# Zero fills of two stages issued in pairs, 2 MB to one transfer, in a DMA-bound decode kernel

## The chip, the cores and the metric

The kernel runs on one core of one Trainium2 chip. Times are device microseconds (us) of that core, the median of several executions; profiles are of one execution each. Every run reported here was classed as undisturbed ("fast"), so like is compared with like. The profile's column PEclk is the share of its full clock that TensorE was granted: 1.00 in most of the stages discussed here, 0.50 in the lines from 330 us on. A transfer's landing time is the time from its issue to its arrival. The backlog is what has been issued and has not landed yet.

## The reference, cut to what matters

One token goes through a conditioned transformer block, and the kernel returns the block's output and the gradients of all ten differentiated inputs. Two of these are large: the gradients of the two key and value caches, of 4 heads x 65,536 rows x 128 each.

```python
def _A_ref(x, k_cache, v_cache, wq, wo):          # Hkv, Sk, Dh = 4, 65536, 128
    W = min(4096, max(256, Sk // 4))              # 4096: only the last 4096 rows are read
    ...
    k = jnp.repeat(k_cache[:, :, Sk - W:, :], rep, axis=1)
    v = jnp.repeat(v_cache[:, :, Sk - W:, :], rep, axis=1)
    ...
def reference(...):
    _out, _vjp = jax.vjp(_f, A_x, A_k_cache, A_v_cache, A_wq, A_wo, B_w_gate, B_w_up, B_w_down, c, w_mod)
    return (_out0, *[jnp.asarray(_g) for _g in _vjp(grad_out)])
```

The first 61,440 rows of each head of both cache gradients are zeros: some 126 MB of the 186 MB that the kernel writes. Those writes are the zero fills.

## The kernel before

The fills are cut into 120 regions of about 1 MB. Eight of them are "narrow", in a shape that leaves out eight rows; the others are plain. The function `zero(n, after)` issues the next n of them on GpSimd's DMA queue, each after some matmul, so that TensorE's progress paces them. Lists say how many are issued at each step of each stage. N and B are the code's names for two stages of large matmuls (tiles n_ps and b_ps below). In B the same queue also carries 1 MB loads of the weight w_mod, and a short step, called ga, makes 64 small matmuls with a part of it.

```python
Z_N = spread(29, 128)                       # N stage: 29 fills over 128 steps
Z_B = spread(29, 43) + [1, 1, 1, 1, 0]      # B stage: 33 fills over 48 chunks
...
    ZW = 4096
    zeros = vt([P, ZW // 2], "zeros", FP8)  # 128 rows x 2 KB of zeros
...
    def zero(n, after=None):
        for _ in range(n):
            ...
            region, narrow_ = zleft.pop(0)
            ...
            else:
                ins = nc.gpsimd.dma_start(out=region.bitcast(FP32), in_=zeros[:, :])
            if after is not None:
                dep(first or ins, after)
...
            for k in range(2):              # N stage, step s of 128
                mm = nc.tensor.matmul(nbank[k][:, :], ...)
            zero(Z_N[s], recent(mm, 6))
...
            for a in range(4):              # B stage, one chunk of 48: 8 matmuls
                for k in range(2):
                    mm = nc.tensor.matmul(bbank[p][k][:, :], ...)
            zero(Z_B[nbq - 1 - len(bq)], recent(mm, 3))
...
    keep[0] = 0
    zero(len(zleft))                        # what is left, at the very end
```

After B comes the FFN loop: seven turns that load weights, form gradients in place, store them, and issue four or more fills each.

## Time and profile before

| | kernel before |
|---|---|
| time, median (lowest to highest) | 607.25 us (607.07 to 607.41), 3 runs |
| span of the profiled run | 605.6 us |
| bytes moved | 248.19 MB, mean 410 GB/s |
| TensorE busy | 388.1 us (64%) |
| N stage, B stage, FFN loop from | 75, 157 and about 293 us |

How to read it: a row such as GB/s of the page cuts the span into 40 slices of 15.1 us. In a kernel that is bound by transfers every slice should be near the best one; a lower slice is time lost, unless its transfers are of a slower kind. The view of stretches gives the same for any cut. The prediction shows these lines for the kernel before, with the waits and the order of GpSimd's instructions.

### The profile page before, as it was taken

To read this page: it belongs to the slowest core of one execution; us is meant where nothing else is said; L and a number is where in the kernel's file an instruction comes from. 1 tells how busy PE (TensorE), PEld (TensorE's weight loads), DVE (VectorE), ACT (ScalarE), POOL (GpSimd) and SP (SyncE) were. 2 spreads that over 40 slices of the span, in tenths; PEclk is the share of its full clock that TensorE was granted. 3 is DMA by queue.
4 is the path that set the end of the run, shared out by engine and by line. 5 is a ranking of instruction groups with operands and counts; after the bars stand their busy time and mean duration, and the time that the engine had idled before them with its cause. 6 is when DMAs were issued, how large, how long until landed. Compare 5 with 4: busy or idle time off the path is not lost.

```text
span 605.6 us, 10906 instructions
## 1 busy us (share of the span) xinstructions
PE 388.1 (64%) x4496; PEld 265.6 (44%) x4516; DVE 325.1 (54%) x616; ACT 282.4 (47%) x426; POOL 177.8 (29%) x281
## 2 busy tenths in 40 slices
PE   3997788999899989989450454344343277757200
PEld 3995434334344446648340353333333256656200
DVE  3754498999511010060462866756667288778420
ACT  3489514557211014228181768558385833764100
POOL 0002121221322212313342464364542523132230
PEclk9999699999999989989755555555555585755555
DMA  8999999999999999999999999999999999999997
GB/s 353 419 417 421 409 426 413 413 419 420 420 425 426 424 426 419 402 425 411 403 412 391 374 396 409 407 416 404 409 414 420 420 423 411 421 424 425 426 416 282
DMA packets 49522, 248.19 MB, mean 410 GB/s; under 512 B 5629, under 2 KB 5629, under 8 KB 29056
## 3 DMA queue, kind: packets, MB, share of 16 engines
q0 software_dynamic: 37792, 210.78, 90.4%
q1 hardware_dynamic: 11632, 36.71, 17.6%
q8 instruction: 35, 0.57, 0.4%
q14 instruction: 15, 0.12, 0.1%
q10 hardware_dynamic: 48, 0.01, 0.0%
HBM read 61.87 MB, written 185.60 MB: 409 GB/s over the span
## 4 chain that ended last, share of the span: by engine, by line
PE 35%; DMA 29%; DVE 17%; ACT 8%; issue 7%; POOL 1%; ACTq 0%; POOLq 0%; another core or an unknown queue 0%; DVEq 0%; SPq 0%
DMA out_dram<-arena 15%; PE b_ps L687 14%; DMA arena<-in_B_w_down_dram 9%; PE n_ps L635 6%; DVE arena L206 4%; DVE arena L193 4%; DMA arena<-in_B_w_gate_dram 3%; DVE arena L210 3%; DVE junk L210 3%; ACT arena L241 2%; PE t_ps L597 2%; DMA arena<-in_B_w_up_dram 2%; PE tp_wq L453 2%; PE w_ps L394 2%; PE tp_k L434 1%
## 5 line engine op out<-in xcount | busy, mean ns | idle before, releaser
L169 POOL DMA_DIRECT2D out_dram<-zeros x112 | 61.6, 550 | 203.8 <-PE q_ps L471 50.4
L687 PE MATMUL b_ps<-arena 128*128 128x512 bf16 x372 | 88.2, 389 | 0.6
L836 PE MATMUL tp_side<-ident_bf,arena 128*128 128x128 bf16 x416 | 50.1, 297 | 50.9 <-ACT arena L837 41.9
L837 ACT COPY arena<-tp_side 128x1024 bf16<-128x1024 bf16 x52 | 52.1, 1010 | 56.6 <-PE tp_side L836 56.4
L193 DVE TENSOR_TENSOR arena<-arena 128x2048 bf16<-128x2048 bf16 x64 | 76.5, 1224 | 2.3 <-PE n_ps L635 0.3
L210 DVE CUSTOM_DVE_ANT_0 arena<-arena,scr 128x1024 bf16<-128x1024 bf16 x56 | 65.2, 1222 | 9.4 <-ACT scr L969 9.4
L635 PE MATMUL n_ps<-arena 128*128 128x512 bf16 x248 | 65.0, 378 | 7.0 <-DVE arena L193 5.1
L836 PEld LDWEIGHTS <-arena 128*128 128x128 bf16 x416 | 41.1, 137 | 56.2 <-issue 56.1
L241 ACT ACTIVATE arena<-scr,h 128x1024 bf16<-128x1024 bf16 x56 | 61.0, 1145 | 0.0
L687 PEld LDWEIGHTS <-arena 128*128 128x128 bf16 x384 | 37.7, 100 | 46.5 <-issue 7.1
L210 DVE CUSTOM_DVE_ANT_0 junk<-arena,b1k 128x1024 bf16<-128x1024 bf16 x28 | 34.3, 1224 | 26.9 <-DMA arena<-in_B_w_down_dram 26.4
L873 POOL DMA_DIRECT2D out_dram<-arena x42 | 30.7, 734 | 45.8 <-ACT arena L241 38.1
L635 PEld LDWEIGHTS <-arena 128*128 128x128 bf16 x256 | 24.6, 97 | 41.8 <-issue 16.4
L1134 ACT ACTIVATE arena<-ps_kv 128x512 bf16<-128x512 f32 x48 | 26.2, 687 | 28.4 <-PE ps_kv L1130 28.2
L599 ACT CAST arena<-t_ps 128x512 bf16<-128x512 f32 x56 | 30.1, 589 | 12.1 <-PE t_ps L597 12.1
L1130 PE MATMUL ps_kv<-junk,arena 8*128 8x128 bf16 x256 | 26.9, 303 | 11.6 <-DVE arena L206 10.3
L949 PE MATMUL fg<-hh_bf,arena 128*128 128x1 bf16 x224 | 8.1, 166 | 40.5 <-DMA arena<-in_B_w_down_dram 38.8
L1130 PEld LDWEIGHTS <-arena 8*128 8x128 bf16 x256 | 25.0, 140 | 13.3 <-issue 13.3
L202 DVE CAST arena<-b_ps 128x512 bf16<-128x512 f32 x5 | 3.5, 692 | 47.1 <-PE b_ps L687 47.1
L949 PEld LDWEIGHTS <-arena 128*128 128x128 bf16 x224 | 7.1, 105 | 43.5 <-DMA arena<-in_B_w_down_dram 41.4
L455 ACT COPY arena<-tp_wq 128x1024 bf16<-128x1024 bf16 x23 | 21.8, 1032 | 8.1 <-PE tp_wq L453 8.1
L206 DVE TENSOR_SCALAR arena<-arena,cs_col 128x4096 bf16<-128x4096 bf16 (+1 forms) x16 | 16.0, 1017 | 8.2 <-DMA out_dram<-arena 8.0
(297 smaller groups left out, 650.7 us busy)
## 6 DMA issues: line engine op xcount, KB each, us to landing
out_dram<-zeros POOLq DMA_DIRECT2D x112, 1024.0 KB, 13.8
out_dram<-arena POOLq DMA_DIRECT2D x32, 1024.0 KB, 18.9
out_dram<-arena POOLq DMA_DIRECT2D x36, 512.0 KB, 9.3
arena<-in_A_wq_dram SPq DMA_DIRECT2D x8, 1024.0 KB, 19.9
out_dram<-zeros POOLq DMA_DIRECT2D x8, 960.0 KB, 12.7
arena<-in_B_w_down_dram SPq DMA_DIRECT2D x14, 512.0 KB, 10.6
out_dram<-arena POOLq DMA_DIRECT2D x28, 256.0 KB, 10.3
arena<-in_A_wo_dram SPq DMA_DIRECT2D x6, 1024.0 KB, 25.0
```

The costliest lines, as they stand in the source:

```text
L169: ins = nc.gpsimd.dma_start(out=region.bitcast(FP32), in_=zeros[:, :])
L193: return nc.vector.tensor_tensor(out=out, in0=a, in1=b, op=op)
L206: return nc.vector.tensor_scalar(out=out, in0=a, scalar1=s1, scalar2=None, op0=op0)
L210: return nc.vector.tensor_tensor_reduce(out=out, in0=w, in1=b, scale=1.0, scalar=0.0, op0=ALU.mult, op1=ALU.add, accum_out=acc)
L241: return nc.scalar.activation(out=out, in_=b, func=ACT.Copy, scale=col)
L599: nc.scalar.copy(out=o, in_=ps)
L635: mm = nc.tensor.matmul(nbank[k][:, :], lhsT=k_nat[:, g, t_ * DH:(t_ + 1) * DH], rhs=vp[:, t_ % 2, 4 * k:4 * k + 4, :].rearrange("p h d -> ...
L687: mm = nc.tensor.matmul(bbank[p][k][:, :], lhsT=a4[:, p, h, :], rhs=wo_t[u][:, a, k * 512:(k + 1) * 512], start=(i == 0 and a == 0), stop= ...
L836: nc.tensor.transpose(tp[:, i * P:(i + 1) * P], blk[:, i * P:(i + 1) * P], ident_bf[:, :])
L837: nc.scalar.copy(out=blk, in_=tp[:, :])
L873: nc.gpsimd.dma_start(out=ug_part(view, q, j0, n), in_=ug_tile(q, k, j0, n))
L1130: nc.tensor.matmul(ps[:, t4 * DH:(t4 + 1) * DH], lhsT=rows[32 * g:32 * g + HG, t_ * P:(t_ + 1) * P], rhs=hd[32 * g:32 * g + HG, :], start= ...
```

## The change

The intent is fewer and larger transfers in the N and B stages. A fill there takes two neighbouring regions when it can, and the lists are cut to 17 and 18 calls.

```diff
-Z_N = spread(29, 128)
-Z_B = spread(29, 43) + [1, 1, 1, 1, 0]
+Z_N = spread(17, 128)
+Z_B = spread(16, 43) + [1, 0, 1, 0, 0]
...
+    def wide_fill(region, i, n):
+        return nc.gpsimd.dma_start(
+            out=region[:, i * ZW:(i + n) * ZW].bitcast(FP32).rearrange("p (t x) -> p t x", t=n),
+            in_=zeros[:, :].rearrange("p (t x) -> p t x", t=1).broadcast_to([P, n, ZW // 2]))
...
-    def zero(n, after=None):
+    def zero(n, after=None, most=1):
...
             else:
-                ins = nc.gpsimd.dma_start(out=region.bitcast(FP32), in_=zeros[:, :])
+                m = 1
+                while m < most and zleft and not zleft[0][1] and zleft[0][0][0] is region and zleft[0][0][1] == i + m:
+                    zleft.pop(0)
+                    m += 1
+                ins = wide_fill(region, i, m)
...
-            zero(Z_N[s], recent(mm, 6))
+            zero(Z_N[s], recent(mm, 6), 2)
...
-            zero(Z_B[nbq - 1 - len(bq)], recent(mm, 3))
+            zero(Z_B[nbq - 1 - len(bq)], recent(mm, 3), 2)
...
-    zero(len(zleft))
+    zero(len(zleft), None, 2)
```

More of the change, by code (lines that the diff above doesn't have):

```diff
@@ L127 @@
             for i in range(region.shape[1] // ZW):
-                zregions.append(region[:, i * ZW:(i + 1) * ZW])
+                zregions.append((region, i))
     narrow = zregions[0:len(NARROW)]
@@ L156, in zero @@
                 return
-            region, narrow_ = zleft.pop(0)
+            (region, i), narrow_ = zleft.pop(0)
             first = None
@@ L165, in zero @@
                 ins = nc.gpsimd.dma_start(
-                    out=region[8:P, :].bitcast(FP32).rearrange("(t p) x -> p t x", t=2),
+                    out=region[8:P, i * ZW:(i + 1) * ZW].bitcast(FP32).rearrange("(t p) x -> p t x", t=2),
                     in_=zeros[0:60, :].rearrange("p (t x) -> p t x", t=1).broadcast_to([60, 2, ZW // 2]))
             else:
-                ins = nc.gpsimd.dma_start(out=region.bitcast(FP32), in_=zeros[:, :])
+                m = 1
[3 more added lines that the diff above has]
+                ins = wide_fill(region, i, m)
             if after is not None:
```

## The prediction

> **What bounds the kernel now.** I read the page's slices first, then the DMA table, the waits, the stretches (busy time and DMA rate by window), the landing times of the fills, and the order in time of GpSimd's instructions. The page:
>
> ```profile
> GB/s 353 419 417 421 409 426 413 413 419 420 420 425 426 424 426 419 402 425 411 403 412 391 374 396 409 407 416 404 409 414 420 420 423 411 421 424 425 426 416 282
> HBM read 61.87 MB, written 185.60 MB: 409 GB/s over the span
> out_dram<-zeros POOLq DMA_DIRECT2D x112, 1024.0 KB, 13.8
> ```
>
> Between start and drain no slice falls below 374 GB/s and the best reach 426, so the transfers bound the whole kernel: 248.19 MB at 426 GB/s would be 583 us of the 605.6 us span. The other 23 us are the start, the drain at the end, one dip, and stages whose mix of transfers runs at about 408. The zero fills are nearly half of the bytes. They depend on no result, so they are the ballast that keeps the queue full while compute has nothing to store. The stretches show where the rate is lost (columns: stretch, length, busy time and count of PE, PE loads, DVE, ACT, POOL, granted clock, DMA share, GB/s):
>
> ```profile
> 170.00:180.00 10.00, 9.95 (x47) 4.54 (x47) 0.08 (x2) 0.00 (x0) 2.65 (x5) 1.00 1.13 427
> 250.00:260.00 10.00, 8.42 (x110) 5.26 (x109) 0.85 (x6) 0.76 (x2) 3.00 (x6) 0.99 1.10 397
> 330.00:340.00 10.00, 4.84 (x64) 3.98 (x63) 8.04 (x18) 3.41 (x4) 5.22 (x8) 0.50 0.87 324
> 340.00:350.00 10.00, 4.33 (x79) 4.00 (x79) 7.88 (x14) 9.95 (x11) 3.27 (x6) 0.50 1.07 394
> ```
>
> The N stage (75 to 157 us) and the B stage (157 to 270 us) are PE-bound and DMA-full at once: 9.95 of 10 us of PE beside 427 GB/s. The dip of 330 to 350 us costs, against 420, 10 x (1 - 324/420) + 10 x (1 - 394/420) = 2.9 us. It lies at the first turn of the FFN loop. The waits of GpSimd, then its order in time at the stage border and at the dip:
>
> ```profile
> POOL out_dram L169 <- PE n_ps L635: 44.5, 20, 3.9
> POOL out_dram L169 <- PE b_ps L687: 36.6, 13, 7.5
> POOL out_dram L169 <- DMA out_dram<-zeros: 29.0, 17, 2.1
> ```
>
> ```profile
> 81.58 0.56 POOL L169 DMA_DIRECT2D out_dram<-zeros  x1 [3.87 <-PE n_ps L635]
> ...
> 187.90 0.53 POOL L169 DMA_DIRECT2D out_dram<-zeros  x1 [2.15 <-DMA out_dram<-zeros]
> ...
> 280.26 0.77 POOL L869 DMA_DIRECT2D arena<-in_B_w_up_dram  x1 [5.88 <-PE fold_ps L882]
> ...
> 306.13 0.72 POOL L859 DMA_DIRECT2D out_dram<-arena  x1 [1.15 <-DMA arena<-in_B_w_gate_dram]
> ...
> 333.43 0.71 POOL L859 DMA_DIRECT2D out_dram<-arena  x1 [9.04 <-DVE arena L206]
> ```
>
> Fills are released by the PE's pace in N and in most of B. The 29.0 us are another wait: in the built program GpSimd's transfers take eight completion semaphores in turn, so a transfer waits until the eighth before it has landed ("slots" below). From 180 to 213 us and from 285 to 306 us that limit holds. A fill issued in N, B or the FFN's start lands 9 to 19 us later; so the queue holds 5 to 8 MB.
>
> **What the Trainium skill says.** "DMA: Bandwidth & Descriptors", section "Anatomy of one DMA — SWDGE (gpsimd) path", fits one transfer as about 2.0 us fixed plus bytes over 436 GB/s, and says that the fixed part is mostly the wait for the write receipt. The trace agrees that it is hidden: fills of 1 MB follow each other every 2.5 us from 185 to 210 us (1.05 MB / 426 GB/s = 2.46 us). So pairing cannot save 2 us per transfer. The same page, "Issuing engines are not separate DMA queues", says that transfers of all engines share the same 16 DMA engines; the trace agrees, as SyncE's 1 MB loads of wo take 25 and 31 us beside the fills in the N stage. Its section "Bandwidth" advises batches of at least 1 MiB; both versions keep to that, so it promises little here.
>
> **The change part by part.**
>
> Removed: I replayed the lists of fills. Before, N calls 29 fills and B 33, plus the unchanged 3 of the ga step: 29 and 36 MB. After, N makes 17 calls (11 pairs, 3 singles, 3 of the narrow kind) = 28 MB, and B makes 18 (13 pairs, 3 singles, 2 narrow) = 31 MB, plus 3. With 2 pairs at the very end this makes 26 pairs, and 86 wide transfers in place of 112. At 0.534 us each that is up to 26 x 0.534 = 14 us less issue time, but GpSimd is busy 29% and off the path: worth 0. Cost inside the DMA engines: I estimate an upper bound from the gap between the page's fabric ceiling of 435 GB/s and the 427 seen with 1 MB fills; if all of that were per transfer, it would be 2% of 2.46 us = 0.05 us, and 26 x 0.05 = 1.3 us gained. I take half, **-0.6 us**.
>
> Unchanged: bytes. Each pair still writes 8 KB pieces from a 2 KB source row; the total of 120 regions stays.
>
> Moved: N and B issue 62 - 59 = 3 MB less, which go to the end (1 MB left over before, 4 MB after). 3 x 1.05 MB / 0.426 = 7.4 us of queue. By itself this is zero: what the queue does not carry at 270 us it carries at 590 us, if it runs dry in neither case. So the sum is made of dry moments:
>
> (a) N start. Before, fills come after steps 4, 8, 13, 17 of the stage; after, at 7, 15, 22. At 82.75 us (step 15) only one fill has been added where two were. The fill at 81.58 us landed 9.1 us later: less 2.0 us fixed and 2.5 us for itself, 4.6 us of queue stood ahead. Without the fill at 77.13 us, and 1.2 us later, that is 4.6 - 2.5 - 1.2 = about 0.9 us when the 2 MB are issued, and they need about a microsecond to begin. A dry moment of 0 to 1 us: **+0.4 us**.
>
> (b) B's end. The fill at 265.23 us landed after 13.5 us, so 9 us of queue stood ahead. After, the backlog is 3 MB = 7.4 us shorter from there: when the loads of gate and up are issued at 280.26 us (landing 11.1 us for 0.5 MB, so about 7.8 us ahead) some 0.4 us are left, and around 270 us it can touch zero. **+0.7 us**.
>
> (c) FFN start. Those loads land about 7 us sooner, but the first matmul that needs them started at 292.85 us, after folds that end at 291.6, so this gains only 1.5 us of compute. More comes from the slots: the first store of w_down's gradient was computed at 300.2 us and issued at 306.13, because eight transfers were outstanding. With a shorter queue it goes at about 299 and lands at about 311 in place of 319; the next w_down load follows it and lands near 321 in place of 329.84. The 10.90 us that VectorE waits there shrink to about 3, as its gates are ready at 318.5. The store that ends the dip goes near 324 in place of 333.4: 9 us sooner, for a queue 7.4 us shorter. Of the dip's 2.9 us I expect 2 back: **-2.0 us**.
>
> (d) FFN and end. Turns of the loop stay DMA-bound (about 25.5 us for 10.5 MB), earlier by 7 to 9 us. The last pairs run as the final drain, so the 3 MB come back there, +7.4 us, which cancels the shorter queue.
>
> Sum: -0.6 + 0.4 + 0.7 - 2.0 = -1.5 us, so 607.25 becomes about **605.7 us**.
>
> **The rivals.** First, the queue runs dry in B or N: lumps of 2 MB, then gaps of up to 8 us (GpSimd waited 7.5 us for the PE around 220 us) on a queue 2 to 7 us shorter. For it: step (b) leaves almost nothing at 270 us, and a dry microsecond is never earned back in a kernel bound by transfers. Against it: the backlog was 12.5 us of landing time even at its lowest in mid B. It would make 608 to 611 us. Second, fewer slots taken: with up to 16 MB instead of 8 MB outstanding, GpSimd never stalls on slots, loads go out on time, and slices of 402 to 411 GB/s in B's end and the FFN start rise to 420. For it: 17 such waits. Against it: while it waits on a slot the queue is full by definition, so nothing is lost there directly. With the whole dip and these slices recovered, 601 to 603 us. Third, pure ballast: all is hidden and the total of bytes decides, 607 us. Fourth, a deeper SWDGE queue starves the loads: in B's middle the same bytes stand ahead of the w_mod loads as before (13 MB by the second of them in both versions, N's 1 MB aside), so I give this little weight.
>
> **Range and chances.** The DMA total fixes the time within about 1%: all losses that I can name in the stages concerned are 3.4 us (dip 2.9, 250 to 260 us 0.5), and the possible new dry moments are of the same size. 8 in 10: 602.3 to 608.9. Faster by over 2% needs 595 us, more than all these losses; slower by over 2% needs 12 us of new dryness. Chances: 0.02, 0.97, 0.01.
>
> **What the profile after would show.** Bytes equal at 248.2 MB. Slots: GpSimd's 29.0 us of waits on earlier fills down to below 12. Step (b): landing times near 265 us of about 7 to 9 us, and gate and up loads at 280 us landing in 4 to 6 us. Step (c): the stretch 320 to 345 us without a 10 us piece below 360 GB/s, and the store of 306.13 us near 299. Step (d): the last fills issued near 585 us with the queue still full, and a drain like today's. Step (a) is wrong if 80 to 90 us stays at 425 GB/s. The sum is wrong if B's end shows a piece below 350 GB/s (first rival), or if the FFN turns take less than 25 us, which would mean that they were bound by waits and not by bytes.

## The result

| | before | changed |
|---|---|---|
| median of 6 runs each | 607.29 us | 612.58 us |
| lowest to highest | 606.51 to 607.41 | 610.16 to 614.35 |
| ratio, 95% interval | | 1.0087, 1.0058 to 1.0115 |
| profiled run: time, span | 607.40, 605.6 us | 610.53, 608.8 us |

The ratio is the mean time of one kernel's fast runs over that of the other's of the same rounds, so it isn't quite the ratio of the medians. The changed kernel is slower by 0.9%, outside the predicted range (602.3 to 608.9). Its runs also scatter over 4.2 us, where those of before lie within 0.9 us. The profile is of one of the quicker runs of the changed kernel, so it shows 3.1 us of the median's 5.3.

The page of the changed kernel, the lines that answer to those of before:

```profile
GB/s 354 419 416 421 405 426 411 412 421 420 421 428 426 423 410 386 404 360 395 395 418 406 385 404 413 406 412 411 410 415 420 424 416 415 424 423 426 420 415 291
HBM read 61.87 MB, written 185.60 MB: 407 GB/s over the span
out_dram<-zeros POOLq DMA_DIRECT2D x60, 1024.0 KB, 11.2
out_dram<-zeros POOLq DMA_DIRECT2D x26, 2048.0 KB, 15.6
```

The bytes are the same. Slices 16 to 20 (228 to 304 us) hold new losses: 386, 404, 360, 395, 395 where before had 419, 402, 425, 411, 403. The stretches of the changed kernel, with the columns of the same view in the prediction:

```profile
220.00:230.00 10.00, 9.56 (x61) 5.32 (x62) 1.73 (x5) 4.45 (x7) 2.24 (x3) 0.83 1.06 387
230.00:240.00 10.00, 10.00 (x100) 5.97 (x99) 0.00 (x0) 4.34 (x5) 1.45 (x2) 1.00 1.06 374
270.00:280.00 10.00, 9.08 (x164) 8.23 (x162) 0.00 (x0) 8.45 (x12) 1.93 (x4) 1.00 1.03 343
330.00:340.00 10.00, 4.50 (x40) 3.75 (x38) 8.57 (x18) 6.60 (x7) 3.70 (x6) 0.50 1.03 381
...
268.00:270.00 2.00, 1.05 (x13) 0.65 (x12) 0.59 (x1) 1.07 (x2) 1.20 (x2) 1.00 0.83 303
270.00:272.00 2.00, 1.55 (x25) 1.31 (x23) 0.00 (x0) 1.91 (x3) 1.17 (x3) 1.00 0.75 147
272.00:274.00 2.00, 1.54 (x22) 1.29 (x22) 0.00 (x0) 2.00 (x4) 0.00 (x0) 1.00 1.06 340
```

From 268 to 274 us the queue ran dry and filled again: (303 + 147 + 340) x 2 us is 1.58 MB where 425 GB/s would have moved 2.55, a loss of 2.3 us. The loss of 220 to 240 us is of another kind: the DMA share stays at 1.06. In pieces of 1 us from 227 to 235 us it is 0.83 to 1.16, at only 254 to 406 GB/s. So the queue was thin there and never quite empty; group 3 comes back to this. The dip of the FFN's first turn is smaller than before (381 for 324), as predicted. GpSimd in order of time, before the two holes and at the FFN's start:

```profile
216.75 0.70 POOL L154 DMA_DIRECT2D out_dram<-zeros  x1 [6.35 <-PE b_ps L696]
226.48 0.78 POOL L347 DMA_DIRECT2D arena<-in_w_mod_dram  x1 [9.03 <-PE b_ps L696]
...
261.90 0.72 POOL L154 DMA_DIRECT2D out_dram<-zeros  x1 [8.31 <-PE b_ps L696]
268.80 0.77 POOL L347 DMA_DIRECT2D arena<-in_w_mod_dram  x1 [6.18 <-PE b_ps L696]
...
300.67 0.72 POOL L868 DMA_DIRECT2D out_dram<-arena  x1 [1.64 <-DVE arena L215]
...
328.24 0.71 POOL L868 DMA_DIRECT2D out_dram<-arena  x1 [6.82 <-DVE arena L215]
```

For 6 to 9 us GpSimd has nothing to issue, as it waits for TensorE's next chunks. The same gaps are there in the kernel before (7.5 us ahead of its fill at 226.37 us), but with more queue behind them. The fill at 261.90 us landed after 10.1 us, at 272.0; nothing went in behind it until 268.80.

The accounts agree. From 220 to 300 us the eight 10 us stretches of before add up to 3312 GB/s and those of the changed kernel to 3108: 204 x 10 us = 2.04 MB, at 420 GB/s 4.9 us lost. From 300 to 350 us the changed kernel moves 60 x 10 us = 0.6 MB more, 1.4 us won back. The difference of 3.4 us is close to the 3.1 us by which the profiled runs differ. Why other runs lose some 2 to 4 us more, this profile doesn't show.

### The profile page after: what moved, and what is told of

Its sections match the earlier page's. It is cut to its first block, busy times and chain, and to the rows that moved or that the text cites.

```text
span 608.8 us, 10875 instructions
## 1 busy us (share of the span) xinstructions
PE 386.7 (64%) x4516; PEld 265.0 (44%) x4516; DVE 325.8 (54%) x616; ACT 282.5 (46%) x426; POOL 169.4 (28%) x255
## 4 chain that ended last, share of the span: by engine, by line
PE 35%; DMA 30%; DVE 17%; ACT 7%; issue 6%; POOL 1%; ACTq 0%; POOLq 0%; DVEq 0%; SPq 0%
DMA out_dram<-arena 15%; PE b_ps L696 14%; DMA arena<-in_B_w_down_dram 9%; PE n_ps L644 6%; DVE arena L215 4%; DVE arena L202 4%; DVE arena L219 3%; DVE junk L219 3%; DMA out_dram<-zeros 2%; PE t_ps L606 2%; ACT arena L250 2%; DMA arena<-in_B_w_gate_dram 2%; PE w_ps L403 2%; PE tp_wq L462 2%; PE tp_k L443 1%
## 5 line engine op out<-in xcount | busy, mean ns | idle before, releaser
L154 POOL DMA_DIRECT2D out_dram<-zeros x86 | 52.0, 606 | 191.3 <-PE q_ps L480 50.9
L662 ACT ACTIVATE arena<-n_ps 128x512 bf16<-128x512 f32 x8 | 4.3, 594 | 34.5 <-PE n_ps L659 34.5
```

The source lines that it names most:

```text
L154: return nc.gpsimd.dma_start(out=region[:, i * ZW:(i + n) * ZW].bitcast(FP32).rearrange("p (t x) -> p t x", t=n), in_=zeros[:, :].rearrang ...
```

## The experiments

Theory: what costs time is the amount. By B's end 3 MB less have been issued, so the queue has no backlog when GpSimd has nothing to issue. Rivals: the 2 MB transfers themselves; their lumpy placing; the queue at the FFN's start and not inside B; TensorE as the bound in B. All results below were correct against the reference. "This" and "before" ran on the same chip within one group.

### Group 1: pairs, lumps or amount

**Every pair split.** The changed kernel, but two transfers of 1 MB at the place of each pair.

```diff
-                ins = wide_fill(region, i, m)
+                ins = wide_fill(region, i, 1)
+                for x in range(1, m):
+                    wide_fill(region, i + x, 1)
```

> The changed kernel, with every pair issued as two 1 MB transfers back to back at the same place: same amounts by stage, same lumps, no 2 MB transfers. Theory (the queue runs dry in B because less is issued, in lumps): it stays slow, 609.5 to 613 us, with dry pieces near 232 us and 271 us. Rival (a 2 MB transfer itself is slower or disturbs the loads): back to 606.5 to 608 us.

Measured: 612.13 us, before 607.2, ratio 1.0084 (1.0061 to 1.0107). The loss stays without any 2 MB transfer in it, with a hole of 308 GB/s from 270 to 280 us. The size of the transfer isn't the cause.

**Fewer single fills.** The kernel before, with the changed kernel's amounts.

```diff
-Z_N = spread(29, 128)
-Z_B = spread(29, 43) + [1, 1, 1, 1, 0]
+Z_N = spread(28, 128)
+Z_B = spread(28, 43) + [1, 0, 1, 1, 0]
```

> The kernel before, with single fills, but 28 in N and 31 in B in place of 29 and 33, as the changed kernel has it; 4 single fills are left for the end. Theory in the form 'the amount does it': 609 to 612 us, a dry piece below 350 GB/s near 270 us. In the form 'the lumps do it': 606.5 to 608.5 us.

Measured: 612.3 us, ratio 1.0084 (1.0062 to 1.0105), scatter 3 us. Without pairs and without lumps, taking 1 MB from N and 2 MB from B costs what the whole change costs. The stretches of this run:

```profile
220.00:230.00 10.00, 8.82 (x57) 4.95 (x58) 2.40 (x10) 3.73 (x6) 1.84 (x3) 0.83 1.11 412
260.00:270.00 10.00, 9.21 (x38) 3.89 (x37) 9.32 (x16) 0.96 (x2) 1.55 (x3) 0.89 0.99 358
270.00:280.00 10.00, 8.92 (x145) 8.07 (x145) 0.00 (x0) 7.97 (x13) 1.85 (x4) 1.00 0.95 311
```

The hole at B's end is there and deeper; the one at 220 to 240 us is almost gone (412, and 414 in the next stretch). So the lumps move some of the loss to the middle of B, but the total is set by the amount.

**Pairs with the amount put back.** 30 MB in N and 33 in B.

```diff
-Z_N = spread(17, 128)
-Z_B = spread(16, 43) + [1, 0, 1, 0, 0]
+Z_N = spread(18, 128)
+Z_B = spread(17, 43) + [1, 0, 1, 0, 0]
```

> The changed kernel with 18 calls in N and 19 in B: 30 and 33 MB in pairs, so 1 MB more by the end of B than before the change, nothing left for the end. If the amount does it: 605 to 608 us and no piece below 390 GB/s near 270 us. If lumps or pairs do it: 609 to 613 us still.

Measured: 607.08 us, ratio 0.9996 (0.9981 to 1.0011). The loss is gone and the pairs are still there; from 270 to 280 us it moves 421 GB/s. One piece, 250 to 260 us, is at 361; it doesn't show in the time.

**The changed kernel again**, unedited, as the anchor.

> The changed kernel again on this chip, as the anchor, and to see whether its spread (610 to 614 us over six runs, against 606.5 to 607.4 before) comes again. Theory: 610 to 614 us, spread over 2 us; a profile taken in a slower run shows longer dry pieces in B than the first profile (2.3 us near 271 us).

Measured: 611.1 us (610.3 to 614.8), ratio 1.0084 (1.0051 to 1.0117). The size of the loss and the scatter repeat. The profile fell on the quickest run again, so the slow runs remain unseen.

### Group 2: how much, and where

**One MB less.** Pairs, 28 MB in N and 33 in B: the changed kernel with one more call in B, `Z_B = spread(17, 43) + [1, 0, 1, 0, 0]`.

> Pairs, 28 MB in N and 33 in B: 1 MB less than before the change by B's end. Theory (only the amount counts, and the kernel before had about 1 MB to spare: 3 MB = 7.4 us of queue cost 5.1 us in the run with fewer single fills): 607 to 608.5 us. Rival (each missing MB costs its 2.46 us, nothing was to spare): 609 to 610 us. Rival (pairs cost something of their own): also above 609 us.

Measured: 607.26 us, ratio 0.9998 (0.9983 to 1.0013). It differs from the changed kernel by one call, so 2 MB, in B alone (the other calls of B move by a step or so), and the whole loss is gone. N's missing megabyte is harmless with B's amount in place.

**Six MB less.** Single fills, 28 in N and 28 in B (`Z_B = spread(25, 43) + [1, 0, 1, 1, 0]` in the kernel before).

> Single fills, 28 MB in N and 28 in B: 6 MB less than before. Theory: 6 x 2.46 = 14.8 us of queue less the 2.3 us to spare, so about 619.5 us (617 to 621), with dry pieces in B far longer. Rival (the FFN's start takes in the gap by starting sooner, so the loss saturates): 611 to 615 us.

Measured: 620.2 us, ratio 1.0213 (1.0186 to 1.0241). The stretches:

```profile
220.00:230.00 10.00, 8.05 (x46) 4.07 (x47) 2.67 (x13) 3.93 (x7) 1.56 (x3) 0.83 0.75 262
270.00:280.00 10.00, 8.14 (x127) 7.26 (x126) 0.08 (x1) 8.22 (x13) 2.37 (x4) 1.00 0.84 280
```

From 3 MB less (612.3) to 6 MB less (620.2) the loss grows by 7.9 us, 2.6 us for each megabyte, about its full price of 2.46 us at 426 GB/s. The loss doesn't saturate.

**Three MB more.** Pairs, 32 MB in N and 33 in B (`Z_N = spread(19, 128)` in the changed kernel), taken from the end.

> Pairs, 32 MB in N and 33 in B: 3 MB more than before by B's end, taken from the end. Theory (a full queue can't gain): 606 to 607.5 us, as the run with 30 and 33 MB. If a thicker cushion also takes away the losses left in 250 to 260 us and 330 to 350 us: 604 to 605.5 us. If loads behind a deeper queue start late: 608 to 611 us.

Measured: 607.31 us, ratio 1.0007 (0.999 to 1.0024). Nothing is gained above the amount of before. This run shows best that TensorE isn't the bound in B. The first matmuls of the FFN loop in order of time, first of the changed kernel, then of this one:

```profile
291.87 1.74 PE L941 MATMUL fg<-h_bf,arena 128*128 128x1 bf16 x64
```

```profile
300.02 0.29 PE L941 MATMUL fg<-h_bf,arena 128*128 128x1 bf16 x4
```

TensorE reaches the FFN 8 us later than in the changed kernel (it also waits 5.0 us for a weight load behind the deeper queue), and the kernel ends 5 us sooner.

**Late.** The changed kernel with the missing 3 MB issued at B's end: `Z_CB = 6` in place of 3.

> The changed kernel with the 3 missing MB issued at the end of B (6 single fills in place of 3 after the last w_mod load), so that the FFN starts behind the same amount as before. If what counts is the queue at the FFN's start: 606.5 to 608 us. If what counts is the dry pieces inside B (near 232 us and 271 us, some 3.4 us in the first profile of the changed kernel), which this can't fill: 609.5 to 612 us.

Measured: 612.58 us, ratio 1.0092 (1.0071 to 1.0113). Adding the bytes behind the holes doesn't help: all six fills go out from 270.13 us, and the hole is there already.

```profile
268.00:270.00 2.00, 1.08 (x5) 0.39 (x4) 1.14 (x2) 1.07 (x2) 0.62 (x1) 1.00 0.94 348
270.00:272.00 2.00, 1.77 (x29) 1.65 (x29) 0.00 (x0) 1.33 (x2) 2.00 (x5) 1.00 0.54 74
272.00:274.00 2.00, 1.38 (x23) 1.14 (x20) 0.00 (x0) 2.00 (x3) 1.32 (x3) 1.00 0.95 334
```

The time is lost inside B, before 274 us. What goes first after the gap is the w_mod load of 269.38 us. In pieces of 1 us the rate from 271 to 275 us is 111, 319, 348 and 283 GB/s, and then 467 as the fills follow.

Together, by the amount issued up to B's end, against the kernel before:

| MB | kernel | median us |
|---|---|---|
| +3 | pairs, 32 and 33 | 607.31 |
| +1 | pairs, 30 and 33 | 607.08 |
| 0 | before, single | 607.2 |
| -1 | pairs, 28 and 33 | 607.26 |
| -3 | pairs (the change), pairs split, single | 611.1 to 612.6, 612.13, 612.3 |
| -6 | single, 28 and 28 | 620.2 |

### Group 3: TensorE's time in B, and the dip of the FFN's first turn

**Tripled small matmuls**, in the kernel before and in the changed one. They write the same result again.

```diff
     mod_tiles(ga_ps, ga_t, range(KD), True)
+    mod_tiles(ga_ps, ga_t, range(KD), True)
+    mod_tiles(ga_ps, ga_t, range(KD), True)
```

> The kernel before, with the 64 small matmuls of the ga step done three times over (same result), so that TensorE takes 3.5 us longer in the middle of B (1.74 us each in the trace). Theory: the queue's cushion at 265 us (about 9 us) hides it: 606.8 to 608.5 us. Rival (TensorE's own time is the bound in B, the transfers follow it): about 610.7 us.

> The changed kernel with the same 3.5 us more of TensorE in B. Theory: with the queue dry, each microsecond of TensorE in B is a microsecond more of the whole, 614.5 to 617 us (3 to 4 us above the changed kernel's 611 to 612.6). Rival (the loss is in the transfers alone): 611 to 613 us.

Measured: 619.18 us (ratio 1.0211, 1.0181 to 1.0242) and 624.49 us (1.0291, 1.0275 to 1.0306). Both went up by about 12 us, so both theories missed: the experiment did something else than planned. TensorE in order of time, the kernel before with the tripled matmuls:

```profile
214.85 2.18 PE L344 MATMUL ga_ps<-cs_bf,arena 128*128 128x1 bf16 x79
227.21 1.10 PE L344 MATMUL ga_ps<-cs_bf,arena 128*128 128x1 bf16 x36 [10.17 <-issue]
```

TensorE stood still for 10.17 us in the midst of the added matmuls, for nothing that the view of waits shows ("issue"). Its next step came at 231.5 us where it was at 216.0: 15.5 us of delay, not 3.5. That is more than either backlog could hide, so the pair tells nothing of the cushion. I did it again in group 4 with wide matmuls. The view of transfers by window has a lead on the stop: in both traces one packet of 16 KB of the queue that the profile calls "instruction" falls into it, at 224.7 us here and at 222.8 us in the changed kernel, each time 2.5 us before TensorE goes on (227.21 and 225.34 us). That fits instructions that came late; it was not tested.

The stop also shows how a queue empties and fills again. GpSimd had nothing to issue for 18.76 us:

```profile
232.04 0.53 POOL L169 DMA_DIRECT2D out_dram<-zeros  x1 [18.76 <-PE tot_ln_mean L255]
```

```profile
226.00:227.00 1.00, 0.00 (x0) 0.00 (x0) 0.00 (x0) 0.00 (x0) 0.00 (x0) 0.50 1.07 401
229.00:230.00 1.00, 1.00 (x4) 0.43 (x3) 0.11 (x1) 0.00 (x0) 0.00 (x0) 0.50 0.50 188
231.00:232.00 1.00, 1.00 (x5) 0.73 (x4) 0.00 (x0) 0.00 (x0) 0.00 (x0) 0.50 0.00 0
232.00:233.00 1.00, 1.00 (x4) 0.32 (x3) 0.57 (x4) 0.00 (x0) 0.53 (x1) 0.55 0.00 0
233.00:234.00 1.00, 1.00 (x6) 0.48 (x5) 0.00 (x0) 0.00 (x0) 0.00 (x0) 1.00 1.02 393
234.00:235.00 1.00, 1.00 (x7) 0.46 (x5) 0.00 (x0) 0.00 (x0) 0.47 (x1) 1.00 1.22 459
...
245.00:246.00 1.00, 1.00 (x11) 0.58 (x9) 0.00 (x0) 0.61 (x1) 0.64 (x2) 1.00 1.03 348
248.00:249.00 1.00, 1.00 (x6) 0.49 (x5) 0.00 (x0) 0.83 (x1) 0.00 (x0) 1.00 0.88 233
```

The rate falls over some five microseconds, and the DMA share with it: I read this as the 16 engines running out one after another. So a backlog loses time before it is empty. The way back is short when a fill goes first: issued at 232.04 us, it moves at 393 GB/s from 233 us and at 459 from 234. It is slow for the two w_mod loads that follow a second gap. From 245 to 251 us they move at 213 to 393 GB/s while the engines count as busy (0.87 to 1.03). The same two loads, behind a full queue in the kernel before, move at 393 to 434 GB/s (234 to 242 us). The slow stretches of the changed kernel and of the late run are such loads too: of the packets, 221 of 222 (231 to 234 us) and 189 of 190 (271 to 274 us) are under 8 KB, the size of the fills' pieces. Why a load is slow there is not shown.

**Fills ahead of the blocked store.** In the FFN's first turn GpSimd waits for VectorE with a store, and the fill behind that store waits too. Here fills go first; with pairs (on the kernel with 28 and 33 MB) and with single fills (on the kernel before: `zero(2)` for the line shown).

```diff
             if q + 2 < NB:
                 load_ug(q + 2, 0, 4)
+            if q == 0:
+                zero(1, None, 2)
             wd_outer(q + 1, 0)
-            zero(z[2])
+            if q > 0:
+                zero(z[2])
```

> Pairs with 28 and 33 MB (607.26 us), and in the first turn of the FFN loop one pair of fills issued ahead of the store that GpSimd waits for (the dip of 330 to 350 us) in place of one single fill behind it. If the dip's 2.9 us are a loss of the whole kernel: 604.5 to 606 us and no piece below 390 GB/s there. If the loop takes them back anyway: 607 to 608 us.

> The kernel before with the same step: in the first turn of the FFN loop two single fills ahead of the store that GpSimd waits for. As the run with pairs: 604.5 to 606 us if the dip is a loss of the whole, 607 to 608 us if not. If slots matter there, it gains less than the run with pairs, as its two fills wait for slots.

Measured over five rounds: 606.52 us (ratio 0.9989, 0.9976 to 1.0001) and 605.91 us (0.9981, 0.9968 to 0.9993), before 606.96. The stretches of the run with single fills:

```profile
330.00:340.00 10.00, 3.76 (x43) 2.92 (x41) 6.85 (x16) 3.30 (x4) 4.55 (x7) 0.50 1.11 414
340.00:350.00 10.00, 4.21 (x75) 3.88 (x75) 8.00 (x14) 9.95 (x11) 3.23 (x6) 0.50 1.07 412
```

The dip of 324 and 394 GB/s is filled. Of its 2.9 us only about 1 shows in the time; in this profile the piece from 250 to 260 us is lower than before (348 GB/s for 397), which would account for 1.2 us of the rest. The single fills are the one version here that is faster than both kernels clear of noise, by 0.2%; the pairs' gain isn't clear of noise.

### Group 4: TensorE's time in B again

Sixteen wide matmuls into an unused tile after the ga step, on the kernel before, on the changed one, and on the one with 3 MB more. The failed step of the prediction is about just this.

```diff
     cp(ga, ga_ps[:, 0:KD])
+    idle = psum.tile([P, 512], FP32, name="idle", tag="mm")
+    for _ in range(16):
+        nc.tensor.matmul(idle[:, :], lhsT=ident_bf[:, :], rhs=wo_t[0][:, 0, 0:512], start=True, stop=True)
```

> The run with tripled small matmuls stalled TensorE for a further 10 us in a way that the profile does not explain (some 15.4 us of delay, not 3.5), so it is done again with 16 wide matmuls into an unused tile after the ga step: 16 x 0.216 us = 3.5 us more of TensorE in B, on the kernel before. Theory: the cushion hides it, 606.8 to 608.5 us. Rival (TensorE's time in B is the bound): 610 to 611 us.

> The changed kernel with the same 3.5 us of wide matmuls. Theory: nothing hides them, 614 to 617 us. Rival: 611 to 613 us.

> Pairs with 32 and 33 MB (607.31 us) with the same 3.5 us of wide matmuls. Theory: hidden behind a thicker cushion, 606.8 to 608 us. If the place of the fills matters and not the cushion: as the kernel before with wide matmuls, or worse.

(The delay of the tripled run was 15.5 us, not the 15.4 of the first of these texts.) This time the delay is as planned: the step after it came at 219.7 us in place of 216.1 on the kernel before, and at 218.2 in place of 214.5 on the changed one.

| on | ratio to before, without | with 3.6 us more of TensorE | difference |
|---|---|---|---|
| before | 1 | 1.0027 (1.0006 to 1.0049), 609.02 us | 1.6 us |
| changed | 1.0084 to 1.0087 | 1.0126 (1.0111 to 1.0141), 614.88 us | 2.5 us |
| 3 MB more | 1.0007 | 1.0023 (1.0009 to 1.0038), 608.59 us | 1.0 us |

The order is the theory's: the thinner the queue, the more of TensorE's delay comes through. But the theory had expected the two with a full queue to hide it all, and they don't (609.02 against 606.8 to 608.5; 608.59 against 606.8 to 608). The kernel before shows a new hole at 250 to 260 us, 324 GB/s where it had 397. So its backlog isn't 9 us thick everywhere: the gap of 5.86 us ahead of the w_mod load (at 249.5 us, here at 253.1) uses it up. The kernel with 3 MB more has such a hole too: 366 and 338 GB/s from 250 to 270 us, where it had 393 and 415 without the delay. The intervals of the three differences, 1.3 to 1.8 us each way, overlap; the grading is likely, not proven.

## Why the prediction was wrong, point by point

**What bounds the kernel** was right: transfers, with equal bytes. In the profiled pair the stretches with a lower rate account for the loss (3.4 us for 3.1).

**The step that failed is (b), B's end, "a backlog 3 MB shorter can touch zero: +0.7 us".** In the profiled run, 260 to 300 us lost 3.0 us (127 x 10 us = 1.27 MB at 420 GB/s). Another 1.9 us went from 220 to 240 us, for which the sum had no term; together they are the 4.9 us above, and the median has 2 us more. Three things were wrong. First, it compared the backlog at two moments, 265 and 280 us, where a fill or load is issued. The queue runs out between issues, in the gaps of 6 to 9 us in which GpSimd waits for TensorE. At the moment of issue nothing is seen of it: the gate and up loads issued from 280.96 us landed after 6.9 to 8.2 us, later than the 4 to 6 foreseen, so the queue stood fuller than predicted, 7 us after the hole. Second, "touching zero" was priced at next to nothing. The late run moved 348, 74 and 334 GB/s in three pieces of 2 us: the queue runs out gradually, and the load that goes first is slow. Third, the same question was asked of the middle of B only in a rival. That rival named the very gap (7.5 us near 220 us), but the prediction set it aside, as 12.5 us of landing time seemed enough; less the 2 us fixed and the fill's own 2.5 us that it counts elsewhere, and 4.9 us for the 2 MB missing by then, 3.1 us were left for a gap of 9 us, and 220 to 240 us fell to 387 and 374 GB/s. The size of the queue was read too large in the same way: landing times of 9 to 19 us, less the 2 us fixed, are 3 to 7 MB at 426 GB/s and not 5 to 8.

**Step (d), that the 3 MB cost nothing as the FFN would run 7 to 9 us sooner**, failed with it. In the last turn of the loop, the last matmul that writes fg from h_bf began at 444.7 us in place of 448.8: 4.1 us sooner. The 7.4 us of fills at the end came in full; 7.4 - 4.1 = 3.3 us is the profiled loss. The single fills with 3 MB less show the same without pairs (445.5 us there, so 7.4 - 3.3 = 4.1 us, and its profiled run lost 4.3).

**Step (a)** was wrong by its own test, without harm: 76 to 88 us stays at 425 GB/s, so the dry microsecond at N's start didn't come. That a transfer needs about a microsecond to begin is borne out by the tripled run (issued at 232.04 us, nothing moved before 233).

**Step (c)** was right in kind and near in size. The first store went at 300.67 us (299 predicted, 306.13 before), the one that ends the dip at 328.24 (324 predicted, 333.43 before), and 1.4 us came back of the 2.0 expected. That the dip's time is worth less to the whole than its size was not foreseen: filled entirely, its 2.9 us gave about 1 us in the run with single fills.

**The saving per transfer** (-0.6 us) can't be seen: three kernels with pairs at 28 to 32 MB in N and 33 in B lie at ratios of 0.9996, 0.9998 and 1.0007, intervals of 0.15 to 0.17% each way, so 1 us. It is neither shown nor refuted.

**The slots** fell as predicted (GpSimd's waits of fills on earlier fills: 29.0 us before, 8.0 after) and gave nothing, as the second rival's counter-argument said. The first rival came true, with its sign of a piece below 350 GB/s at B's end (343 from 270 to 280 us); its size, 608 to 611 us, was also short.

**Open**: the scatter of 4 us. The kernels with 3 or 6 MB less scatter by 3 to 4.5 us, those with 1 MB less or with more by 1.5 us at most (1.9 to 2.6 us when TensorE is delayed in group 4). The clocks give a lead. Take each run's time and mean granted clock against the mean of its own batch. Over the 26 runs of kernels with 3 or 6 MB less the two go together (correlation -0.80, some 2.9 us more for each 0.01 of clock less); over the 30 runs of the kernel before in the four groups they don't (-0.04). That fits TensorE losing some time to the throttle, which a backlog hides. It is a correlation and not an experiment: no profile fell on one of the slowest runs, and group 4 supports only the second half of it.

## What to carry to other kernels

Where bytes that depend on nothing fill the DMA queue beside a compute-bound stage, the number that matters is how much is queued when the issuing engine has its longest gap; write down the backlog at the end of each gap, not at the issues. When you repack such transfers, keep the amount issued up to each point: here 1 MB less cost nothing (pairs), 3 MB less cost 5 us whatever the size of the transfers, and 6 MB less 13 us (single fills). An engine that runs earlier proves nothing: TensorE reached the FFN at 291.87 us in the changed kernel, at 292.85 in the kernel before, and at 300.02 in the one with 3 MB more, which lost nothing.

## What the Trainium skill lacked or had wrong

- "DMA: Bandwidth & Descriptors", section "Bandwidth", advises batches of at least 1 MiB, and its table still gains from there, from 341 GB/s at 1 MB to 425 at 16 MB. It doesn't say that a full queue takes this gain away: here fills of 1 MB run at 427 GB/s (170 to 180 us of the kernel before), and the kernel with 30 and 33 MB, which has 26 pairs of 2 MB in place of 52 single fills, changed by less than about 1 us (607.08 us against 607.2).
- No page has how a load runs behind a thin or emptied queue: here w_mod loads moved at 213 to 393 GB/s with the engines busy (245 to 251 us of the tripled run), and at 393 to 434 behind a full queue. A fill that went first after a gap was at 459 GB/s within 3 us of its issue.
- No page has the backlog that a paced DMA queue needs: here 3 MB less of it (7.4 us of transfers) cost 5 us of 607, and 3 MB more gained nothing.
- "Runtime: NRT & Kernel Launch", section "Instruction fetch mechanics", says that instruction fetch is hidden. That may not hold for many small matmuls in a row: of 192, TensorE stood still for 10.17 us after 156, and an instruction packet of 16 KB came 2.5 us before it went on. Whether fetching is the cause was not tested; 16 wide matmuls at the same place caused no such stop.
